# Copying q two banks at a time, building two constants in fewer steps, and running head 0's PV as one loop, in a decode attention and FFN kernel

## The chip, the cores and the metric

The kernel runs on one core of one Trainium2 chip. The metric is the device time of one execution in microseconds.

## The reference, cut to what matters

One token goes through an attention block with a cache and, beside it, a gated FFN:

```python
xn = layernorm(x)                                  # x: 1 x 640
q = xn @ wq                                        # 32 heads of 128
scores = q . k_cache * 128 ** -0.5                 # k_cache: 32 heads x 32768 x 128, bf16
o = softmax(scores) @ v_cache                      # v_cache: the same size
out = x + o @ wo + (silu(xn @ w_gate) * (xn @ w_up)) @ w_down
```

K and V of a head are 8.39 MB each, so 537 MB of the 554 MB that are read are cache. Every byte of it is used once. There is no way to read less.

## The kernel before

The cache goes through a ring of three slots in SBUF, in the order K0 K1 V0 K2 V1 K3 V2 ... The SyncE (SP) queue issues a load as soon as the slot's former owner is done:

```python
for u in units:                      # wq, k0, k1, v0, k2, v1, k3, ...
    s = slot_of[u]                   # position modulo 3
    if s in owner:
        e.wait_ge(*owner.pop(s))     # wq: PE's q matmuls; k: PE's scores; v: PE's PV
    ...
        e.dma_start(ring[:, s, :], kv_src(A_k_cache, u[1], 0, NJ)).then_inc(s_slot[s], 16)
        owner[s] = (s_qk, NHF * (u[1] + 1))
    ...
        e.dma_start(ring[:, s, :], kv_src(A_v_cache, u[1], 0, NJ)).then_inc(s_slot[s], 16)
        owner[s] = (s_pv, u[1] + 1)
```

For each head VectorE (DVE) multiplies K by q in place, PE sums the products over groups with an identity matrix (`scores`), DVE reduces, and a small exchange between DVE and PE (`turn`, `spread`) finds the maximum. ScalarE (ACT) takes the exponential, and PE multiplies with V (PV). The PV of the head before is used to fill PE's waits in the exchange:

```python
def head(h):
    scores(h)
    if h >= 1:
        total(h - 1)
        pv_part(h - 1, 0)            # 16 matmuls
    turn(h)
    if h >= 1:
        pv_part(h - 1, 1)            # 16
    spread(h)
    if h >= 1:
        pv_part(h - 1, 2)            # 32
    if h >= 2:
        fold(h - 2)
```

Heads 2 to 31 run in a hardware loop of three heads a step, in which PV is straight code. Heads 0 and 1 stand in front of it, and there head 0's PV (issued within head 1) is itself a small hardware loop, four matmuls a step, once in each part:

```python
with t.Fori(0, n // (RUN * W)) as b:             # RUN = 4, W = 4
    for r in range(RUN):
        t.matmul(O, lhsT=P[:, h % PR, bass.ds(b * (RUN * W) + j, W)],
                 rhs=flat[:, bass.ds(b * (RUN * W * DH) + (s * CE + j * DH), W * DH)], ...)
```

The other two parts that the change touches are the copies of q out of PSUM, one bank each (`for b in range(NQB): a.wait_ge(s_q, b + 1); a.activation(out=qb[...512], in_=bank[b], func=Copy)`), and two constants on GpSimd (POOL), `blk` and `fold32`, by nine small steps. Both constants are first used in the tail.

## Time and profile before

| | before |
|---|---|
| time, median of 3 runs | 1286.12 us (1286.08 to 1286.26) |
| profiled span | 1284.9 us |
| read | 554 MB at 431 GB/s |
| from one K issue to the next, mean of 27 (one K and one V, 16.78 MB) | 38.72 us, 433 GB/s |

From the page of the kernel before: busy time of each engine with its share of the span, then two rows of the 40 slices (the DMA engines' busy tenths, and GB/s).

```profile
PE 1042.9 (81%) x5160; PEld 261.2 (20%) x3240; DVE 672.2 (52%) x409; ACT 52.1 (4%) x139; POOL 2.6 (0%) x18
...
DMA  9999999999999999999999999999999999999998
GB/s 424 424 441 433 430 431 441 428 433 433 437 433 428 445 426 435 428 441 428 433 443 428 433 430 441 428 433 435 435 433 430 443 426 435 433 437 433 428 427 370
```

The DMA row is the one that never drops before the last slice. The page's chain of waits is less clear. It gives only half of the span to the DMA:

```profile
## 4 chain that ended last, share of the span: by engine, by line
DMA 53%; PE 29%; DVE 12%; issue 5%; SPq 0%; DVEq 0%
```

The chain goes back from each K load to the PE work that freed its slot, so PE appears in it whether or not the queue had other work at that moment. To tell, one looks at when loads are issued. This is the timeline of SP's queue in the kernel before, from V of head 0 to K of head 4 (start, duration of the issue, line):

```profile
26.30 0.33 SPq L240 DMA_DIRECT2D ring<-in_A_v_cache_dram  x1
56.16 0.33 SPq L231 DMA_DIRECT2D ring<-in_A_k_cache_dram  x1
79.75 0.33 SPq L240 DMA_DIRECT2D ring<-in_A_v_cache_dram  x1
94.50 0.33 SPq L231 DMA_DIRECT2D ring<-in_A_k_cache_dram  x1
114.54 0.33 SPq L240 DMA_DIRECT2D ring<-in_A_v_cache_dram  x1
129.18 0.33 SPq L231 DMA_DIRECT2D ring<-in_A_k_cache_dram  x1
```

K of head 3, issued at 94.50, is multiplied from 132.32 on: 37.8 us, of which the transfer takes about 19.4 (an estimate: 8.39 MB at the measured 433 GB/s).

### The profile page before, as it was taken

To read this page: it belongs to the slowest core of one execution; us is meant where nothing else is said; L and a number is where in the kernel's file an instruction comes from. 1 tells how busy PE (TensorE), PEld (TensorE's weight loads), DVE (VectorE), ACT (ScalarE), POOL (GpSimd) and SP (SyncE) were. 2 spreads that over 40 slices of the span, in tenths; PEclk is the share of its full clock that TensorE was granted. 3 is DMA by queue.
4 is the path that set the end of the run, shared out by engine and by line. 5 is a ranking of instruction groups with operands and counts; after the bars stand their busy time and mean duration, and the time that the engine had idled before them with its cause. 6 is when DMAs were issued, how large, how long until landed. Compare 5 with 4: busy or idle time off the path is not lost.

```text
span 1284.9 us, 10032 instructions
## 1 busy us (share of the span) xinstructions
PE 1042.9 (81%) x5160; PEld 261.2 (20%) x3240; DVE 672.2 (52%) x409; ACT 52.1 (4%) x139; POOL 2.6 (0%) x18
## 2 busy tenths in 40 slices
PE   3599777789787798778798877898787798778797
PEld 1021112221112221112221112221112221112227
DVE  0855665445664446664446664446654446654451
ACT  2000000000000000000000000000000000000000
POOL 0000000000000000000000000000000000000000
PEclk9799888898888898888998888998888998888995
DMA  9999999999999999999999999999999999999998
GB/s 424 424 441 433 430 431 441 428 433 433 437 433 428 445 426 435 428 441 428 433 443 428 433 430 441 428 433 435 435 433 430 443 426 435 433 437 433 428 427 370
DMA packets 10987, 554.16 MB, mean 431 GB/s; under 512 B 1247, under 2 KB 1504, under 8 KB 1760
## 3 DMA queue, kind: packets, MB, share of 16 engines
q1 hardware_dynamic: 10974, 554.00, 99.8%
q8 instruction: 9, 0.15, 0.0%
q14 instruction: 2, 0.02, 0.0%
q10 hardware_dynamic: 2, 0.00, 0.0%
HBM read 553.99 MB, written 0.00 MB: 431 GB/s over the span
## 4 chain that ended last, share of the span: by engine, by line
DMA 53%; PE 29%; DVE 12%; issue 5%; SPq 0%; DVEq 0%
DMA ring<-in_A_k_cache_dram 51%; PE ps L358 16%; DVE ring L577 12%; PE ps L310 10%; DMA ring<-in_A_wo_dram 2%; PE ps L342 1%; PE ps L329 1%; PE ps L400 0%; PE ps L394 0%; PE ps L388 0%; PE ps L451 0%; SPq L253 0%; DVEq L577 0%; DVE sc L583 0%; DVE pmax L589 0%
## 5 line engine op out<-in xcount | busy, mean ns | idle before, releaser
L577 DVE TENSOR_TENSOR ring<-ring,qb 128x8192 bf16<-128x8192 bf16 x128 | 557.8, 4421 | 314.9 <-DMA ring<-in_A_k_cache_dram 314.9
L310 PE MATMUL ps<-ring,ident 128*128 128x512 bf16 x1920 | 499.6, 419 | 0.0
L358 PE MATMUL ps<-ring,P 128*4 128x512 bf16 x1920 | 429.0, 379 | 0.0
L329 PE MATMUL ps<-ring,ident 128*128 128x512 bf16 x128 | 56.1, 439 | 218.5 <-DVE ring L577 217.9
L358 PEld LDWEIGHTS ps<-ring,P 128*4 128x4 bf16 x1920 | 158.2, 85 | 230.1
L329 PEld LDWEIGHTS ps<-ring,ident 128*128 128x128 bf16 x128 | 12.6, 99 | 617.0 <-DVE ring L577 357.3
L583 DVE TENSOR_REDUCE sc<-ps 128x64 f32<-128x512 f32 x128 | 82.3, 685 | 64.0 <-PE ps L310 64.0
L595 DVE TENSOR_SCALAR negb<-ps 128x1 f32<-128x1 f32 x32 | 5.1, 159 | 108.4 <-PE ps L400 108.4
L503 ACT ACTIVATE P<-sc,negb 128x256 bf16<-128x256 f32 x32 | 16.2, 507 | 957.2 <-DVE negb L595 957.2
L592 DVE TENSOR_REDUCE m<-ps 1x1 f32<-1x128 f32 x32 | 8.9, 278 | 85.2 <-PE ps L394 85.2
L380 PEld LDWEIGHTS ps<-identf,o 4*128 4x128 f32 x248 | 30.7, 190 | 13.1 <-issue 13.1
L380 PE MATMUL ps<-identf,o 4*128 4x1 f32 x248 | 33.3, 251 | 0.0
L388 PEld LDWEIGHTS ps<-rsum,ones 128*128 128x128 f32 x64 | 12.1, 190 | 100.1 <-issue 99.2
L494 ACT ACTIVATE o<-ps,rzb 4x512 f32<-4x512 f32 x31 | 21.0, 677 | 6.3 <-PE ps L345 6.3
L301 PE MATMUL ps<-ring 128*128 x40 | 10.3, 425 | 11.4 <-DMA ring<-in_A_wq_dram 11.4
L499 ACT ACTIVATE ocol<-ps 128x1 f32 (+1 forms) x31 | 5.4, 173 | 222.4 <-PE ps L380 222.4
L342 PE MATMUL ps<-ring,P 128*4 x64 | 14.3, 379 | 0.0
L589 DVE TENSOR_REDUCE pmax<-sc 128x1 f32<-128x256 f32 x32 | 13.4, 420 | 0.0
L394 PE MATMUL ps<-identf,pmax 128*1 128x128 f32 x64 | 12.2, 272 | 1.2 <-DVE pmax L589 1.2
L400 PE MATMUL ps<-m,ones 1*128 1x1 f32 x64 | 12.1, 256 | 0.4 <-DVE m L592 0.4
L400 PEld LDWEIGHTS ps<-m,ones 1*128 1x128 f32 x64 | 9.4, 183 | 14.0 <-issue 13.3
L565 DVE RECIPROCAL rzb<-ps 128x1 f32<-128x1 f32 x32 | 5.1, 158 | 8.1 <-PE ps L388 8.1
(75 smaller groups left out, 97.2 us busy)
## 6 DMA issues: line engine op xcount, KB each, us to landing
ring<-in_A_v_cache_dram SPq DMA_DIRECT2D x2, 4096.0 KB, 36.5
ring<-in_A_wq_dram SPq DMA_DIRECT2D x1, 5120.0 KB, 15.6
ring<-in_A_wo_dram SPq DMA_DIRECT2D x3, 1280.0 KB, 24.2
ring<-in_B_w_gate_dram SPq DMA_DIRECT2D x1, 2160.0 KB, 22.6
ring<-in_B_w_up_dram SPq DMA_DIRECT2D x1, 2160.0 KB, 27.5
ring<-in_B_w_down_dram SPq DMA_DIRECT2D x1, 2080.0 KB, 31.2
ring<-in_A_wo_dram SPq DMA_DIRECT2D x1, 800.0 KB, 28.3
ring<-in_A_k_cache_dram SPq DMA_DIRECT2D x32, 41.5
```

Of the source, the lines that this page charges most:

```text
L310: return t.add_instruction(mybir.InstMatmult(start_tensor_calc=False, stop_tensor_calc=stop, tile_size=(128, 128), tile_position=(0, 0), l ...
L329: t.matmul(ob, lhsT=ident[:, :], rhs=src, start=True, stop=False)
L342: t.matmul(O, lhsT=P[:, h % PR, bass.ds(b * (RUN * W) + j, W)], rhs=flat[:, bass.ds(b * (RUN * W * DH) + (s * CE + j * DH), W * DH)], star ...
L358: mm = t.matmul(O, lhsT=P[:, h % PR, j:j + W], rhs=ring[:, s, j * DH:(j + W) * DH], start=(j == 0), stop=(j + W == NJ))
L380: mm = t.matmul(fold_ps, lhsT=o4[:, m * DH:(m + 1) * DH], rhs=identf[0:W, m:m + 1], start=(m == 0), stop=(m == W - 1))
L394: t.matmul(misc[0:1, 0:128], lhsT=pmax[:, h % SR:h % SR + 1], rhs=identf[:, :], start=True, stop=True).then_inc(s_t, 1)
L400: t.matmul(misc[:, 128:129], lhsT=ones[0:1, :], rhs=m1[0:1, h % SR:h % SR + 1], start=True, stop=True).then_inc(s_b, 1)
L494: a.activation(out=o4[:, :], in_=O, func=ACTF.Copy, scale=rzb[0:W, h % SR:h % SR + 1]).then_inc(s_o4, 1)
L503: a.activation(out=P[:, h % PR, :], in_=sc[:, :], func=ACTF.Exp, bias=negb[:, h % SR:h % SR + 1], scale=c_scale, accum_out=rsum[:, h % SR: ...
L577: v.tensor_tensor(out=kh, in0=kh, in1=q[:, None, :].to_broadcast([128, HF, DH]), op=ALU.mult).then_inc(s_mul, 1)
L583: v.tensor_reduce(out=sc[:, i * HF:(i + 1) * HF], in_=bank[i].rearrange("p (j e) -> p j e", e=G), axis=AX.X, op=ALU.add).then_inc(s_red, 1)
L589: v.tensor_reduce(out=pmax[:, h % SR:h % SR + 1], in_=sc[:, :], axis=AX.X, op=ALU.max).then_inc(s_max, 1)
```

## The change

The intent is fewer instructions on ScalarE, GpSimd, VectorE and PE. The diff, cut to its core:

```diff
-                for a in range(RB):
-                    done(g.tensor_copy(out=fold32[a * 32:(a + 1) * 32, :], in_=ident[...]))
-                for a in range(RB):
-                    done(g.memset(blk[a * 32:(a + 1) * 32, a:a + 1], 1.0))
+                done(g.memset(blk[:, :], 1.0))
+                done(g.affine_select(out=blk[:, :], ... pattern=[[-32, RB]], channel_multiplier=1))
+                done(g.affine_select(out=blk[:, :], ... pattern=[[32, RB]], channel_multiplier=-1))
+                for a in range(1, RB):
+                    done(g.tensor_tensor(out=fold32[:, :], ... op=ALU.add))
 ...
+                def pv_whole(h):
+                    s = slot_of[("v", h)]
+                    pv_ready(h)
+                    t.matmul(O[:, 0:1], lhsT=zero[:, :], rhs=zero[:, 0:1], start=True, stop=False, ...)
+                    with t.Fori(0, NJ // (RUN * W)) as b:
+                        for r in range(RUN):
+                            t.matmul(O, lhsT=P[:, h % PR, bass.ds(b * (RUN * W) + r * W, W)], rhs=flat[...], ...)
+                    t.matmul(O[:, 0:1], lhsT=zero[:, :], rhs=zero[:, 0:1], start=False, stop=True,
+                             ...).then_inc(s_pv, 1)
 ...
+                    parts = [] if group[0] is None else range(len(PARTS))
+                    if parts:
                         pv_part(h - 1, 0)
                     turn(h)
-                    if h >= 1:
+                    if parts:
                         pv_part(h - 1, 1)
                     spread(h)
-                    if h >= 1:
+                    if parts:
                         pv_part(h - 1, 2)
+                    elif h >= 1:
+                        pv_whole(h - 1)
 ...
-                for b in range(NQB):
-                    a.wait_ge(s_q, b + 1)
-                    a.activation(out=qb[:, b * 512:(b + 1) * 512], in_=bank[b], func=ACTF.Copy).then_inc(s_qc, 1)
+                for b in range(0, NQB, 2):
+                    a.wait_ge(s_q, b + 2)
+                    a.activation(out=qb[:, b * 512:(b + 2) * 512], in_=banks[:, b * 512:(b + 2) * 512],
+                                 func=ACTF.Copy).then_inc(s_qc, 2)
 ...
-                    if group[0] is None:
-                        v.wait_ge(s_qc, min(NQB, (h * DH) // 512 + 1))
```

The cut leaves out one thing: VectorE also loses its two waits for the q copies, in front of heads 0 and 1. In the big loop PV keeps its three parts. Only head 0's PV is now one loop, placed after head 1's exchange.

More of the change, by code (lines that the diff above doesn't have):

```diff
@@ L271, in pool @@
                                          pattern=[[-1, 128]], channel_multiplier=1))
-                done(g.memset(blk[:, :], 0.0))
-                for a in range(RB):
-                    done(g.tensor_copy(out=fold32[a * 32:(a + 1) * 32, :],
-                                       in_=ident[a * 32:(a + 1) * 32, a * 32:a * 32 + OC]))
-                for a in range(RB):
-                    done(g.memset(blk[a * 32:(a + 1) * 32, a:a + 1], 1.0))
-                assert n[0] == 6 + 2 * RB
+                done(g.memset(blk[:, :], 1.0))
+                done(g.affine_select(out=blk[:, :], in_=blk[:, :], compare_op=ALU.is_ge, fill=0.0, base=0,
+                                     pattern=[[-32, RB]], channel_multiplier=1))
+                done(g.affine_select(out=blk[:, :], in_=blk[:, :], compare_op=ALU.is_ge, fill=0.0, base=31,
+                                     pattern=[[32, RB]], channel_multiplier=-1))
+                for a in range(1, RB):
+                    done(g.tensor_tensor(out=fold32[:, :], in0=fold32[:, :] if a > 1 else ident[:, 0:OC],
+                                         in1=ident[:, a * 32:a * 32 + OC], op=ALU.add))
+                assert n[0] == 11
             @block.tensor
@@ L332, in scores, with pv_ready @@
                         mm.then_inc(s_qk, 1)
-                def columns(h, s, first, n):
-                    if first == 0:
-                        t.matmul(O[:, 0:1], lhsT=zero[:, :], rhs=zero[:, 0:1], start=True, stop=False,
-                                 skip_group_check=True)
-                    with t.Fori(0, n // (RUN * W)) as b:
+                def pv_ready(h):
+                    wait(s_exp, h, lambda h: h + 1)
+                    wait(s_o4, h, lambda h: h)
+                    wait(s_slot[slot_of[("v", h)]], h, lambda h: 16 * use_of[("v", h)])
+                def pv_whole(h):
+                    s = slot_of[("v", h)]
+                    pv_ready(h)
+                    t.matmul(O[:, 0:1], lhsT=zero[:, :], rhs=zero[:, 0:1], start=True, stop=False,
+                             skip_group_check=True)
+                    with t.Fori(0, NJ // (RUN * W)) as b:
                         for r in range(RUN):
-                            j = first + r * W
-                            t.matmul(O, lhsT=P[:, h % PR, bass.ds(b * (RUN * W) + j, W)],
-                                     rhs=flat[:, bass.ds(b * (RUN * W * DH) + (s * CE + j * DH), W * DH)],
+                            t.matmul(O, lhsT=P[:, h % PR, bass.ds(b * (RUN * W) + r * W, W)],
+                                     rhs=flat[:, bass.ds(b * (RUN * W * DH) + (s * CE + r * W * DH), W * DH)],
                                      start=False, stop=False, skip_group_check=True)
-                    return t.matmul(O[:, 0:1], lhsT=zero[:, :], rhs=zero[:, 0:1], start=False,
-                                    stop=(first + n == NJ), skip_group_check=True)
+                    t.matmul(O[:, 0:1], lhsT=zero[:, :], rhs=zero[:, 0:1], start=False, stop=True,
+                             skip_group_check=True).then_inc(s_pv, 1)
                 def pv_part(h, part):
@@ L350, in pv_part @@
                     if part == 0:
-                        wait(s_exp, h, lambda h: h + 1)
-                        wait(s_o4, h, lambda h: h)
-                        wait(s_slot[s], h, lambda h: 16 * use_of[("v", h)])
+                        pv_ready(h)
                     first = sum(PARTS[:part])
-                    if group[0] is None:
-                        mm = columns(h, s, first, PARTS[part])
-                    for j in range(first, first + (PARTS[part] if group[0] is not None else 0), W):
+                    for j in range(first, first + PARTS[part], W):
                         mm = t.matmul(O, lhsT=P[:, h % PR, j:j + W], rhs=ring[:, s, j * DH:(j + W) * DH],
@@ L467, in pe @@
                 hidden_part(0)
-                t.wait_ge(s_const, 6 + 2 * RB)
+                t.wait_ge(s_const, 11)
                 t.wait_ge(s_ob, 1)
@@ L570, in head @@
                     kv = ring[:, s, :].rearrange("p (j d) -> p j d", d=DH)
-                    if group[0] is None:
-                        v.wait_ge(s_qc, min(NQB, (h * DH) // 512 + 1))
                     wait(s_slot[s], h, lambda h: 16 * use_of[("k", h)])
@@ L596, in head @@
                                     scalar2=None, op0=ALU.mult).then_inc(s_neg, 1)
-                v.wait_ge(s_qc, 1)
+                v.wait_ge(s_qc, 2)
                 for h in range(H0):
@@ L620, in dve @@
                                 scalar2=None, op0=ALU.mult).then_inc(s_ov, 1)
-                v.wait_ge(s_const, 6 + 2 * RB)
+                v.wait_ge(s_const, 11)
                 v.wait_ge(s_ov, H + 1)
```

## The prediction

> **What bounds the kernel now.** The DMA queue. The page's slices show the DMA engines at 9 tenths in 39 of 40 slices; it read 554 MB at 431 GB/s over the span. PE is busy 81%, DVE 52%, ACT 4%. In the timeline of SP's queue, K loads follow each other every 38.72 us (129.18 to 1174.60 us, 27 steps); a step carries one K and one V head, 16.78 MB: 433 GB/s. [...] only some 1 us before the first byte and 3 us after the last is anything else.
>
> The chain of waits also names PE, DVE and 5% "issue". I don't read that as work that limits: it runs through whatever freed a buffer, but K loads take 41.5 us from issue to landing and V loads 36.8, for a transfer of 19.4 us at that rate. Each is issued 17 to 22 us before the queue reaches it. That is the slack.
>
> **What the change does.**
> 1. q copies: 8 ACT copies of 0.597 us become 4 of 1024 columns. [...] The first begins at 19.4 us instead of 18.3, the last ends at 27.35 instead of 26.91. The first multiply starts at 35.01, when K of head 0 has landed: 7 us of slack. V of head 0 is issued (26.30) on PE's matmuls, not on the copies. Worth 0.
> 2. Constants: nine steps for blk and fold32 (done at 4.5 us) become six (memset, two affine selects at the traced 0.29, three adds of about 0.2, estimated like the traced copies), done about 4.2. First used at 1262. Worth 0.
> 3. Head 0's PV: two zero matmuls fewer, but it now follows head 1's max exchange instead of filling its waits. Before, 79.8 to 94.3 us. Now pmax is ready at 80.9, the exchange done at 82.2, PV ends about 96.2. The issue of head 3's K, which waits for it, moves from 94.5 to about 96.4. The queue is then busy with V of head 1 until about 112.6: 16 us of slack left. PE is free before head 2's first product (97.8). Head 1's exponential comes 5 us earlier; nothing uses that.
> 4. Two waits of VectorE on values long reached: 0.
>
> On the critical path: nothing. From head 2 on, and in the tail, the programs are the same.
>
> **Prediction.** 1286.1 us, as before; 8 times in 10 between 1285.1 and 1287.1, for the difference of one build from another. Faster by over 2%: 0.005; within 2%: 0.99; slower: 0.005.
>
> **What would show it.** Four ACT copies near 1.02 us; head 3's K issued at about 96.4; later K issues within 1 us of before; K step still 38.7 us; 431 GB/s; DVE's idle time before multiplies about 315 us in all, still ended by K loads; the last wo piece landing near 1281.4.
>
> **What would make it wrong.** A DMA rate that changes with the build (more instruction fetches, say), which would show as other than 431 GB/s; a gap in the queue after 94 us, which needs over 25 us to make 2%; or a wait for the constants at 1262 us that I misread.

The sum for a q copy of 1024 columns came to 1.02 us; only the 0.597 us of a copy of 512 columns is traced in before, the rest was the author's estimate. The 19.4 and 27.35 us in point 1 follow from the 1.02; after shows copies of 1.023 us. That the middle can't go faster was not shown; measured are 433 GB/s from 40 to 1240 us, with the DMA engines busy for all of it (share 1.00).

## More of the kernel before

Last, head 0's PV by its source line, with PE's weight loads and matmuls, and the register steps of PE's sequencer (the rows PEldq), each with first and last start:

```profile
L342 PEld LDWEIGHTS ps<-ring,P x64: 80/85/85, 79.8 to 93.9; 128*4 x64
L342 PE MATMUL ps<-ring,P x64: 376/379/379, 79.8 to 94.1; 128*4 x64
L342 PEldq FUSED_REGOPS  x60: 51/74/79, 76.7 to 93.8; - x60
L342 PEldq ALU_OP  x4: 36/36/36, 76.6 to 79.9; - x4
```

The last row matters later: the sequencer is in the loop at 76.6 us, PE only at 79.8.

## The result, and the profile after

| | before | after |
|---|---|---|
| median, in the same rounds (4 runs each) | 1286.19 us | 1286.11 us (1286.06 to 1286.22) |
| ratio, 95% interval | | 0.9999 (0.9982 to 1.0016) |
| profiled span | 1284.9 us | 1284.8 us |
| from one K issue to the next, mean of 27 from head 4's on | 38.72 us | 38.70 us |
| q copies | 8 of 0.597 us | 4 of 1.023 us |

All ratios here are the mean time of one kernel's fast runs over that of the other's fast runs of the same rounds, so not quite the ratio of the medians quoted. The time is the same.

The page after, same lines: POOL has three instructions fewer, ACT four, PE two; the DMA rows stay.

```profile
PE 1045.3 (81%) x5158; PEld 261.0 (20%) x3238; DVE 672.3 (52%) x409; ACT 51.4 (4%) x135; POOL 2.5 (0%) x15
...
DMA  9999999999999999999999999999999999999998
GB/s 424 424 451 425 428 435 439 428 431 443 431 428 431 445 428 431 439 433 428 431 445 428 433 433 439 428 431 443 431 428 431 445 428 431 439 433 428 433 426 369
```

SP's queue after:

```profile
26.59 0.33 SPq L240 DMA_DIRECT2D ring<-in_A_v_cache_dram  x1
55.97 0.33 SPq L231 DMA_DIRECT2D ring<-in_A_k_cache_dram  x1
79.55 0.33 SPq L240 DMA_DIRECT2D ring<-in_A_v_cache_dram  x1
99.45 0.33 SPq L231 DMA_DIRECT2D ring<-in_A_k_cache_dram  x1
114.69 0.33 SPq L240 DMA_DIRECT2D ring<-in_A_v_cache_dram  x1
129.33 0.33 SPq L231 DMA_DIRECT2D ring<-in_A_k_cache_dram  x1
```

One row moves: K of head 3 is issued 4.95 us later (99.45 for 94.50). The next rows are within 0.2 us of before, and no later load is more than 0.5 us away. K of head 3 is multiplied from 132.18 us on, in before from 132.32: it came 5 us later into the line and left it at the same moment. So the change did something that is worse by 5 us, and the line took it up.

It is also more than the prediction had put (96.4). Head 0's PV by its source line after:

```profile
L349 PEld LDWEIGHTS ps<-ring,P x64: 80/80/81, 81.9 to 98.9; 128*4 x64
L349 PE MATMUL ps<-ring,P x64: 376/377/379, 82.0 to 99.0; 128*4 x64
L349 PEldq FUSED_REGOPS  x48: 74/74/79, 82.0 to 98.7; - x48
L349 PEldq ALU_OP  x16: 36/36/36, 81.9 to 98.3; - x16
```

From first to last start the 64 matmuls now take 17.0 us, before 14.3. The sequencer takes about the same time in both, 17.2 us (76.6 to 93.8) and 16.8 us (81.9 to 98.7). Before, it was 3.2 us ahead of PE (76.6 against 79.8), because PE was still working off the scores, until 79.7 us; after, the lead is gone (81.9 against 82.0): the loop stands behind `spread`, which waits for DVE, and PE has nothing else left to do. By what means the sequencer gets ahead no trace shows; only the lead is measured.

The constants were ready at 4.3 us (before 4.5) and are used from 1262 us on.

### The profile page after: what moved, and what is told of

It is laid out like the page before. It is cut to its first block, busy times and chain, and to the rows that moved or that the text cites. A ratio compares the mean times of both kernels' runs of the same rounds, so it can differ in the third digit from the quotient of the medians.

```text
span 1284.8 us, 10022 instructions
## 1 busy us (share of the span) xinstructions
PE 1045.3 (81%) x5158; PEld 261.0 (20%) x3238; DVE 672.3 (52%) x409; ACT 51.4 (4%) x135; POOL 2.5 (0%) x15
## 4 chain that ended last, share of the span: by engine, by line
DMA 52%; PE 28%; DVE 13%; issue 7%; DVEq 0%; SPq 0%
DMA ring<-in_A_k_cache_dram 50%; PE ps L361 16%; DVE ring L583 13%; PE ps L312 8%; DMA ring<-in_A_wo_dram 2%; PE ps L349 1%; PE ps L331 1%; PE ps L403 0%; PE ps L397 0%; PE ps L391 0%; PE ps L458 0%; DVE sc L589 0%; SPq L253 0%; DVEq L583 0%; DVE pmax L595 0%
## 5 line engine op out<-in xcount | busy, mean ns | idle before, releaser
L312 PE MATMUL ps<-ring,ident 128*128 128x512 bf16 x1920 | 499.2, 419 | 0.0
L361 PE MATMUL ps<-ring,P 128*4 128x512 bf16 x1920 | 429.0, 379 | 0.0
L331 PE MATMUL ps<-ring,ident 128*128 128x512 bf16 x128 | 55.9, 436 | 213.5 <-DVE ring L583 212.9
L331 PEld LDWEIGHTS ps<-ring,ident 128*128 128x128 bf16 x128 | 12.6, 99 | 611.3 <-issue 321.0
```

The lines of the kernel that those rows point to most:

```text
L312: return t.add_instruction(mybir.InstMatmult(start_tensor_calc=False, stop_tensor_calc=stop, tile_size=(128, 128), tile_position=(0, 0), l ...
L331: t.matmul(ob, lhsT=ident[:, :], rhs=src, start=True, stop=False)
L361: mm = t.matmul(O, lhsT=P[:, h % PR, j:j + W], rhs=ring[:, s, j * DH:(j + W) * DH], start=(j == 0), stop=(j + W == NJ))
```

## The experiments

Theory: the DMA queue binds, each part of the change has slack, and the only thing that moved on the path to a load (head 0's PV) stayed within its slack. First rival: gain and loss cancel, a real gain at the start against the slower PV. Second rival: the chain of waits is to be taken at face value, and PE work in front of an issue counts in full. All kernels gave a result that passed the comparison with the reference.

### One part of the change at a time

Run 1 is before with the q copies, the constants and the removed DVE waits, and PV in three parts. Run 2 is the other half, only PV as one loop.

```diff
 # e1_copies_consts: before plus
+ a.activation(out=qb[:, b * 512:(b + 2) * 512], ...)     # and the constants, the waits
 # e2_pv_only: after minus the same
- a.activation(out=qb[:, b * 512:(b + 2) * 512], ...)     # and the constants, the waits
```

> Before with the q copies, the constants and the two VectorE waits changed, head 0's PV left in three parts. Theory (the DMA queue binds, everything changed has slack): 1286.1 us within 0.4, K of head 3 issued at 94.5 us as before, four copies of 1.02 us, V of head 0 issued at 26.3 to 26.6. Rival (the change has a real gain of 1 us or more in the start that the slower PV of head 0 gives back): 1285.1 us or less.

> After with the q copies, constants and VectorE waits undone, so only head 0's PV as one loop. Theory: 1286.1 us within 0.4, K of head 3 issued at about 99.4 us, PV of head 0 from about 82 to 99 us as in after. Rival (gain and loss cancel in after): 1287 us or more.

| | time, median of 4 | before, same rounds | K of head 3 issued |
|---|---|---|---|
| copies and constants alone | 1286.25 us | 1286.19 us | 94.32 |
| PV alone | 1286.21 us | 1286.19 us | 99.95 |

Both ratios are 1.0 (0.998 to 1.002). Neither half gains or loses 0.1 us in the medians, so there is no pair of effects that cancel. The first rival falls.

### How much slack K of head 3 has

Matmuls with zero weights behind head 0's loop add nothing to the result and hold up the release of the slot by about 0.215 us each (30.9 us for 144).

```diff
+                    for r in range(48):                      # 32 and 144 in the other two
+                        t.matmul(O, lhsT=zero[:, :], rhs=ring[:, s, ...], start=False, stop=False, ...)
                     t.matmul(O[:, 0:1], lhsT=zero[:, :], rhs=zero[:, 0:1], start=False, stop=True, ...)
```

> After with 48 more PV matmuls of zero weights behind head 0's loop (right result), about 10.3 us more PE work before K of head 3 can be issued: issue at about 109.8 us. Theory: the queue is busy with V of head 1 until about 112.7 us (landing of head 3's K at 132.05 less 19.4 of transfer), so the time stays 1286.1 within 0.5. Rival (the chain of waits taken at face value, where PE holds 28%: PE work in front of an issue counts in full): 1296 us.

> The same with 144 zero matmuls, about 31 us: K of head 3 issued at about 130.3 us. Theory: only the part beyond the slack counts: the queue runs dry at about 112.7, so the gap is about 18 us plus 1 to 2 of first-byte time: 1304 to 1307 us, and a hole in the DMA rate from about 113 to 132 us. Rival: plus 31 us, 1317.

After these two, a third with a smaller dose:

> After with 32 zero matmuls, about 6.9 us: K of head 3 issued at about 106.5 us. From the runs with 48 and 144 (landing of that K 2.3 and 20.8 us later than in after, for issues 11.0 and 30.9 us later) the slack is between 8.7 and 10.1 us from 99.45. Theory: still inside it, 1286.1 us within 0.5. Rival (every late issue costs something, 2.3 us for 11 of delay in proportion): 1287.6.

| zero matmuls | K of head 3 issued | multiplied from | time, median of 4 | before, same rounds |
|---|---|---|---|---|
| 0 (after) | 99.45 | 132.18 | 1286.11 us | 1286.19 us |
| 32 | 106.38 | 132.64 | 1286.28 us | 1286.47 us |
| 48 | 110.44 | 134.45 | 1288.47 us | 1286.19 us |
| 144 | 130.35 | 152.98 | 1307.86 us | 1286.19 us |

A delay of 6.9 us costs nothing, one of 11.0 costs 2.3 us, one of 30.9 costs 21.7. Up to some point delay is free, beyond it it counts about in full: from 48 to 144 matmuls, 19.9 us more delay (130.35 less 110.44) gave 19.4 us more time. That is slack, not a share of the work, and the second rival falls (it had 10 and 31 us).

The size of the slack was not what was expected: the 48 missed its forecast of no loss, and the 144, at 1307.86 us, came out above its 1304 to 1307. In the windows of the run with 144 one sees the queue run dry (the last two columns are the DMA share and GB/s; the late K is issued at 130.35):

```profile
105.00:110.00 5.00, 5.00 (x25) 1.96 (x23) 5.00 (x2) 0.00 (x0) 0.00 (x0) 1.00 0.97 419
110.00:115.00 5.00, 5.00 (x25) 1.96 (x23) 1.23 (x1) 0.00 (x0) 0.00 (x0) 1.00 0.03 13
115.00:120.00 5.00, 5.00 (x24) 1.96 (x23) 0.00 (x0) 0.00 (x0) 0.00 (x0) 1.00 0.01 3
120.00:125.00 5.00, 5.00 (x25) 1.99 (x24) 0.00 (x0) 0.00 (x0) 0.00 (x0) 1.00 0.00 0
125.00:130.00 5.00, 5.00 (x25) 1.99 (x24) 0.00 (x0) 0.00 (x0) 0.00 (x0) 1.00 0.00 0
130.00:135.00 5.00, 5.00 (x25) 0.21 (x3) 0.69 (x1) 0.68 (x1) 0.00 (x0) 1.00 1.10 419
```

It was empty from about 110 us on, not 112.7. The first bytes of the late K moved between 131 and 132 us (0 GB/s from 130 to 131, 983 in the next), 0.7 to 1.7 us after its issue; the expectation had put 1 to 2. The forecast took the landing of a load and subtracted 19.4 us, but a load that finds the queue empty needs longer from issue to landing. K of head 3 took 23.9 us in the run with 48 and 22.5 us in the run with 144 (the minima in the two rows below, in this order), so to be in time for 132.18 it has to be issued by 108.3 to 109.7. The slack left in after is thus some 9 to 10 us, and 48 zero matmuls overran it.

```profile
DMA to landing us min/median/max: 23.9/41.5/52.7
...
DMA to landing us min/median/max: 22.5/41.5/52.4
```

Counting bytes agrees: wq and five cache loads up to V of head 1 are 47.2 MB, at 433 GB/s 109 us, plus about 1 us before the first byte. That is an estimate, but it would have given the right point before any run. The median of 41.5 shows that later K loads still wait for their turn as before.

### Taking the queue out of the way

If the queue hides the change, the change must show where the queue doesn't bind. In these kernels all K and V loads from head 2 on move half of their columns (V of the last head stays whole); the engines do the same work, on partly old data. The result is wrong in its arithmetic; it still passed the comparison, which says that this comparison is blind to such an error.

```diff
-                        e.dma_start(ring[:, s, :], kv_src(A_k_cache, u[1], 0, NJ)).then_inc(s_slot[s], 16)
+                        n = NJ if u[1] < 2 else NJ // 2
+                        e.dma_start(ring[:, s, 0:n * DH], kv_src(A_k_cache, u[1], 0, n)).then_inc(s_slot[s], 16)
```

and the same for V. First before and after so cut:

> Before, with the K and V loads of heads 2 to 30 cut to half their bytes (K of head 31 also; wrong result on purpose, all engine work unchanged). Theory (the DMA queue binds): with about 19.4 us of transfer for a head instead of 38.7 the engines become the limit, PE first (1043 us busy): 1070 to 1190 us. If instead the chain through PE and DVE were the limit, the time would stay above 1260.

> After, with the same half loads. Theory: the lost 5 us in the release of the slot after head 0 (K of head 3 issued at 99.45 for 94.50) is no longer hidden by a full queue, so this is slower than the half-load kernel before by 2 to 6 us. Rival (the change is worth nothing wherever it is): equal within 0.5 us. Second rival (fewer instructions help once the queue is out of the way): faster by 1 us or more.

Then the copies and constants alone, and after with head 0's PV as straight code (see the next section):

> Half loads again, with the q copies, constants and waits changed and head 0's PV as in before. Theory (in the half-load pair only the PV's later end cost the 5 us): 1009.9 us within 1, like the half-load kernel before. Rival (the copies or constants cost or gain something once the queue is out of the way): outside that by more than 1 us.

> Half loads, after with head 0's PV as 64 straight matmuls in the late place. Of the 5 us, the loop's pace should be worth about 3.3 (K of head 3 issued at 96.1 for 99.45) and the place the rest: 1011 to 1012.5 us. Rival (it is all the place): 1015.

| half loads | time, median of 4 | ratio to before, full loads | K of head 3 issued |
|---|---|---|---|
| before | 1009.91 us | 0.7850 | 94.74 |
| copies and constants alone | 1009.65 us | 0.7846 | 94.39 |
| after, PV as 64 straight matmuls | 1011.15 us | 0.7859 | 95.84 |
| after | 1015.05 us | 0.7893 | 99.28 |

Before and after were run on another chip and in other rounds than the two rows between them, so differences of a few tenths of a microsecond across these pairs mean nothing.

The first row says that the queue was the limit: with 306.5 MB to read instead of 554 (30 of the 32 K loads and 29 of the V loads halved), 276 us go. The page of this run (before, half loads) shows PE in the queue's old place:

```profile
PE 971.4 (96%) x5160; PEld 260.8 (26%) x3240; DVE 671.7 (67%) x409; ACT 52.1 (5%) x139; POOL 2.6 (0%) x18
...
## 4 chain that ended last, share of the span: by engine, by line
PE 92%; DVE 3%; DMA 3%; issue 1%; ACT 0%; DVEq 0%
```

The forecast of 1070 us and more was too high, because it took PE's 1043 us of busy time as fixed. It fell to 971: the mean granted TensorE clock that the records give (1 is the most they show) rose from 0.889 to 0.977. The pages place the fall: the score matmuls, which follow each wait for K, went from 499.6 to 439.8 us of busy time (L310 and L312), while PV's stayed at 429.0 (L358 and L360). In before one can see how: after a wait of 4.60 us for DVE, PE's score matmuls from 63.09 us on start 0.427 us apart at a granted clock of 0.50, until about 66.5 us, and 0.216 apart at 1.00 from 67 us on. So PE's 1043 us had itself been stretched by such waits: before each quarter's first score matmul they came to 218.5 us in all (L329), with half loads to 17.6 (L331). A run of before in the last batch points the same way by chance: its mean granted clock was 0.747, and with the full loads it took only 1.2 us more than the median (1287.65 against 1286.45 us).

The other rows say what the change is worth once nothing hides it. The copies and constants: nothing (1009.65 against 1009.91 us). The PV: a loss, 5.1 us in the medians and 4.1 in the profiled spans (1013.1 against 1009.0; runs of these kernels scatter by 0.5 to 2 us). Straight PV code in the same late place gets back 3.9 of the 5.1 us. So the larger part of the loss is the loop's pace, the rest its place.

The path of the loss is not the one that the forecast named, a late release of the slot. K of head 3 landed at nearly the same time in both half-load kernels, at 113.1 us in before and 113.4 in after (issue plus the 18.4 and 14.1 us to landing), and in neither run did DVE wait for a K load after head 2's. The loss goes through PE, which passes from head 0's PV to head 2's scores without a pause. Here are the end of PV, the first score matmul of head 2 and the first product with K of head 3, in before and then in after:

```profile
94.54 0.17 PE L347 MATMUL ps<-zero 128*4 128x1 bf16 x1
94.71 0.39 PE L331 MATMUL ps<-ring,ident 128*128 128x512 bf16 x1
117.00 17.43 DVE L579 TENSOR_TENSOR ring<-ring,qb 128x8192 bf16<-128x8192 bf16 x4
...
99.08 0.17 PE L354 MATMUL ps<-zero 128*4 128x1 bf16 x1
99.26 0.39 PE L333 MATMUL ps<-ring,ident 128*128 128x512 bf16 x1
121.05 17.43 DVE L585 TENSOR_TENSOR ring<-ring,qb 128x8192 bf16<-128x8192 bf16 x4
```

From there on the 4.1 us of the profiled spans stay.

### Why one loop is slower than three

Theory: PE's sequencer sets the pace of the loop, 1.10 us for a step of four matmuls (81.7 to 98.2 us from the first to the last register step of the loop line, over 15 steps), while PE needs 4 x 0.215 = 0.86. A lead over PE hides that for a while; in the late place there is no lead. The rows of the loop line, in after (first two), with eight matmuls a step, and in the early place:

```profile
L347 PEldq FUSED_REGOPS  x16: 78/78/78, 81.7 to 98.2; - x16
L347 PEldq COMPARE_BRANCH  x16: 76/208/214, 82.6 to 99.0; - x16
...
L347 PEldq FUSED_REGOPS  x8: 78/78/78, 82.1 to 94.2; - x8
...
L347 PEldq FUSED_REGOPS  x16: 78/78/78, 76.4 to 92.8; - x16
```

Three kernels, one look each: eight matmuls a step; straight code in the late place; the one loop moved ahead of `turn`.

```diff
 # e7_run8
-    RUN = 4
+    RUN = 8
 # e8_unrolled
-                    with t.Fori(0, NJ // (RUN * W)) as b: ...
+                    for j in range(0, NJ, W):
+                        t.matmul(O, lhsT=P[:, h % PR, j:j + W], rhs=ring[:, s, j * DH:(j + W) * DH], ...)
 # e9_early
                         pv_part(h - 1, 0)
+                    elif h >= 1:
+                        pv_whole(h - 1)
                     turn(h)
 ...
                         pv_part(h - 1, 2)
-                    elif h >= 1:
-                        pv_whole(h - 1)
```

> After with 8 instead of 4 matmuls in one step of head 0's PV loop (8 steps instead of 16). Theory on the slower PV (17.3 us for 64 matmuls): PE's sequencer needs 1.09 us for a step of 4, of which about 0.32 (loop test, register sum, the first register step) is paid once a step; so 8 steps of about 1.86: PV ends near 97 us, K of head 3 issued at about 97.2. Rival (the cost is per matmul, or PE's clock): still about 99.4. Total time 1286 in both.

> After with head 0's PV as 64 straight matmuls in the same place. Theory: without loop and register steps the sequencer is ahead of PE, 0.215 us a matmul as in the heads of the big loop: PV 13.9 us, K of head 3 issued at about 96.1, which is what the prediction had put (96.4). Rival (place, not the loop, makes it slow): about 99.4.

> After with head 0's one loop moved ahead of head 1's max exchange, right behind its scores. Theory on the slower PV (PE's sequencer needs 1.09 us for a loop step and in before had a start of about 3 us on PE, gained while PE worked off the scores): the sequencer starts the loop at about 76.5 us as in before, so PV ends near 94 and K of head 3 is issued at about 94.1, while head 1's exponential moves from 82.1 to about 95 us. Rival (one loop of 16 steps is itself slower than three): K of head 3 at 97 or later. Total time 1286.2 in both.

| | PV, first to last start | sequencer in the loop from | K of head 3 issued | time, one run |
|---|---|---|---|---|
| before, three loops | 79.8 to 94.1 | 76.5 | 94.50 | |
| after, one late loop of 4 | 82.0 to 99.0 | 81.7 | 99.45 | |
| late, 8 a step | 82.4 to 97.7 | 82.1 | 98.08 | 1286.29 us |
| late, straight | 82.1 to 95.7 | | 96.14 | 1286.40 us |
| early, one loop of 4 | 79.7 to 93.7 | 76.4 | 94.12 | 1286.47 us |

Straight code:

```profile
L348 PE MATMUL ps<-ring,P x64: 376/379/379, 82.1 to 95.7; 128*4 128x512 bf16 x64
```

It gives what the prediction had put, 96.1 for the K issue. So the place alone costs 1.6 us (1.9 were predicted), and the loop's pace in that place 3.3 us more. Before, in the same rounds, had medians of 1286.33 us (first two) and 1286.47 us (the last), so the time is the same in all three. The early loop has its 3 us of lead and ends as in before, though it is the same single loop: it isn't the number of loops. With eight matmuls a step the sequencer's step is 1.73 us (94.2 less 82.1 over 7 steps). Two equations, 1.10 for 4 and 1.73 for 8, give 0.16 us a matmul and 0.47 us a step. With eight a step the sequencer is thus just level with PE (0.216 us a matmul against 0.215); by this estimate still longer steps should bring it under, which no run tried.

That run came out at 98.08, not at 97.2. Its first eight or so matmuls went at half speed, as the timeline of weight loads shows:

```profile
84.38 0.13 PEld L349 LDWEIGHTS ps<-ring,P 128*4 x1 [0.30 <-issue]
84.81 0.13 PEld L349 LDWEIGHTS ps<-ring,P 128*4 x1 [0.30 <-issue]
85.23 0.13 PEld L349 LDWEIGHTS ps<-ring,P 128*4 x1 [0.30 <-issue]
```

They start 0.427 us apart. This is the distance that the score matmuls of before, also of 512 columns, had at a granted clock of 0.50 (63.5 to 66.5 us, above), where 0.216 was measured at 1.00. The clock rows of the pages agree: the third of the 40 slices, 64 to 96 us, has 8 tenths in this run and 9 in after, and in after the clock is 1.00 from 82 to 86 us. Why it was low in this run and not in after, whose waits in the exchange were as long (1.21 us for `pmax` in both, then 0.67 and 0.66 for `m`), no run shows.

## Why the prediction was right

- **The limit.** "The DMA queue" was right: 433 GB/s in both kernels (40 to 1240 us), half the bytes take 276 us off, and a delay of K of head 3's issue cost nothing at 6.9 us and 2.3 us at 11.0, when the queue had run empty.
- **The parts of the sum.** q copies, constants and waits "worth 0": shown twice, under full loads (1286.25 for 1286.19 us) and with the queue out of the way (1009.65 for 1009.91, not in the same rounds). The copies took 1.023 us, put at 1.02. Their times were put early: the first at 19.4 began at 20.18, the last ended at 27.68 and not 27.35. Nothing waits for them before K of head 0 at 34.8 us.
- **Head 0's PV.** The mechanism was right (later, within slack), the size was off. The step that failed is "PV ends about 96.2". It took the loop's matmuls at PE's pace, 0.215 us, and missed that in before the sequencer, at 1.10 us for four, was hidden by a lead of 3.2 us. PV ended at 99.2, the issue came at 99.45. With it "PE is free before head 2's first product (97.8)" failed too: PE turned to head 2 at 99.43, in before at 97.89. That was made up within head 2, whose scores wait for DVE: V of head 2 was issued at 114.69 for 114.54.
- **The slack.** "16 us of slack left", with the queue busy "until about 112.6", was too much. The queue is dry at about 110 and an empty queue's load takes 22.5 to 23.9 us, so a K issued at 96.4 would have had some 12 to 13 us, and the real issue had 9 to 10. The conclusion stood because 5 us of delay was still well inside it. Had PV ended 11 us later still, it would have cost 2.3 us, as the run with 48 zero matmuls shows.
- **The signs to look for.** Later K issues within 1 us (at most 0.5), the K step 38.70 us, 431 GB/s: as put. DVE's idle time before multiplies rose from 314.9 to 320.0 us and not "about 315": head 1's exchange, done 5 us earlier, lets DVE wait longer for K of head 2 (11.39 us instead of 5.71).

No run was faster than before by more than its scatter, and none pointed to a version that would be: the queue moves 433 GB/s with no drop before the last slice, and all that is left outside it is about 1 us at the start and 3 us at the end.

## What to carry to other kernels

When one queue is full from end to end, ask of every change only one thing: does a load get issued later than the moment when the queue would run empty? The chain of waits doesn't answer that, since it follows whatever freed a buffer (here it gave PE 28 to 29%, and 6.9 us more of PE's work in front of an issue cost nothing); the issue times, set against bytes over rate, do. A change that is free under a full queue may still be a loss: here the cleaner loop costs 4 to 5 us as soon as the queue isn't the limit, because this hardware loop, standing behind a wait, started without a lead (0.1 us instead of 3.2) and ran at its sequencer's pace (1.10 us for four matmuls), which is slower than PE's (0.86).
